# Attention with its row maxima shared between a front stage and the attention steps: 96 units in front in place of 80, and two maxima a step from step 171 on

## The chip, the cores and the metric

The kernel runs on one core of a Trainium2 chip. The time is the device time of one execution in microseconds, the median of several runs. Beside it stands the profile of one execution, whose span reaches from the program's first instruction to its last.

## What is computed

Two attention layers over the same input `x` (2048 tokens of 448 values, 16 heads of 28) and a gate that mixes them:

```
g = sigmoid((x * gate_w).sum(-1))
a = linear attention: phi(q) (phi(k)^T v) / (phi(q) phi(k)^T 1), phi = two softmaxes over a learned map
b = softmax(q k^T / sqrt(28)) v, all 2048 keys for every query
out = g * (a @ A_wo) + (1 - g) * (b @ B_wo)
```

The change is about layer b. Its softmax subtracts from every score the largest score of its query and head (the row maximum), so that the exponentials stay in range.

## The kernel before

**Order of the work.** The kernel writes out by hand the order of every instruction of TensorE (PE), VectorE (DVE), ScalarE (ACT) and GpSimd (POOL); each engine works through its own list in order. Transfers go through SyncE's queue (SP) and through scratch tensors in device memory. The stages are: the projections of queries and keys of layer b (`proj_qk`), the keys and values of layer a by tiles of 128 tokens (key stage, t = 0 to 15 of the loop at line 703), the queries of layer a and their products (the same loop, q = t - 16 from 0 on), the values of layer b (`value_b`, eight tiles in that loop from q = 18 on, eight behind it at line 926), and the attention of layer b (loop at line 1136).

**Attention.** There are 4 groups of 4 heads and 4 blocks of 512 queries, 16 pairs `gq` in all, and 16 tiles of 128 keys for each: 256 steps `s`. In a step `scores` (line 880) computes for each of the four heads a tile of 128 keys by 512 queries, in three passes (line 863; high and low parts of the numbers). The four heads lie in four groups of 32 rows of the PE array, so that four such matmuls run side by side. ACT turns each into exponentials (line 871). `values` (line 1001) multiplies the exponentials of two steps ago with the values (line 1008), eight passes that all run on all 128 rows. The row maximum enters the scores through an extra row of the query tile, so the maxima of a pair must be there before its first step: `load_nm` puts them there about four steps ahead.

**The row maxima** come from a cheaper computation of the same scores, and in two ways:

- *In the front*, `mx_unit` (line 238). A unit takes 128 queries, two heads and 1024 keys: four matmuls (line 260), in the four row groups; two give differences of the scores of two key tiles (`pmd`), two the scores of one of them (`pmb`). ACT takes the positive part of a difference (line 264), DVE adds it to the other score and takes the maximum over the row (line 265): two instructions on each. 16 units make a pair `gq`. A unit also issues the loads of what later units need: at certain units `pair_query` and `pair_load` (four and six transfers; the latter has a subtraction on POOL, taken up by `take_subs`), and towards the end `mx_query` and `mx_load`, the plain tiles for the second way.
- *In attention*, for the pairs that the front has left: the list `flats` (line 275), one item for 128 queries, one head and 512 keys. `mx_next` hands a step some items; `mx_score` (line 288) is one matmul of 28 rows in the row group of its head, `mx_done` one reduction on DVE (line 295). A unit of the front so replaces four items.

The split is `NF`, the number of units in front: 80 units do pairs 0 to 4; the other eleven pairs are 704 items, three to a step.

**Where the units stand in front** (80): one each in the last four of the `proj_qk` units; in the key stage, one at the start of each pair of tiles and three more from `tick`, which counts the matmul passes of the key and value tiles and starts a unit at each mark of `pace["at"]`; one at the start of iterations q = 0, 1 and of all from q = 8 on (line 747); a second at the end of iterations q = 19 to 25 (line 797); one at line 924; and the rest (`rest`, 15 units), spread over the 77 passes of value tiles 8 to 14. Banks: PSUM has eight, of 128 x 512 values. In the loop, units have four from q = 2 on, and six from the end of q = 22 on (`psn[1]`); a unit takes four of them.

**Banks in attention.** One bank is for the values, seven go round in `scores` by the list `free`. The order in which they are handed on to the next step is written there, one way for three maxima and another for any other number:

```
    if len(todo) == 3:
        b = free[:]
        free[:] = [b[2], b[0], b[3], b[1], b[6], b[4], b[5]]
        st, pm = {e0: b[0], e1: b[1], l0: b[4], l1: b[5]}, [b[2], b[3], b[6]]
    else:
        n = 4 + len(todo)
        b = free[:n]
        free[:] = free[n:] + b[4:] + b[:4]
        st, pm = dict(enumerate(b[:4])), b[4:]
```

`st` are the banks of the four scores, `pm` those of the maxima. With three maxima, the first passes of two heads (e0, e1) go out beside the maxima of the two others (l0, l1), whose scores follow one pass later. In the other branch the scores' passes come first, heads 0 to 3 in each, and the maxima last.

Of the kernel before, what the change touches and what calls it, by code (L numbers as in the profile page):

```python
# [24 lines left out]
NT = S // P  # L25
# [1 line left out]
SCALE = DH ** -0.5  # L27
EPS = 1e-6
NU = NG * NQ * 16
NF = 80  # L30
LOWEST = -3.0e38
LAG = 2
OUTS = (200, 238, 246, 210)
# [8 lines left out]
def gated_mix_kernel(ctx, tc, xT, wqkB, wvB, wvA, wkAT, wqAT, phi, woA, woB,  # L42
# [20 lines left out]
    def ps_s(nm):  # L63
        return ps.tile([P, 512], F32, tag="s", name=nm, bufs=psn[0])
# [4 lines left out]
    def ps_mx(nm):  # L69
        return ps.tile([P, 512], F32, tag="mx", name=nm, bufs=psn[1])  # L70
# [113 lines left out]
    def mx_load(g, c):  # L184
        mxs[("kc", g, c)] = mx_rows(mx_tile("kc", f"kc{g}_{c}", 5), range(4), k_d[g], range(4),
                                    c * 512)

    def mx_query(gq):
        g, qb = divmod(gq, NQ)
        mxs[("qc", gq)] = mx_rows(mx_tile("qc", f"qc{gq}", 3), range(4), q_d[g], range(4), qb * 512)  # L190
# [19 lines left out]
    def pair_query(gq, hp):  # L210
        g, qb = divmod(gq, NQ)
        mxs[("qp", gq, hp)] = mx_rows(mx_tile("qc", f"qp{gq}_{hp}", 3), range(4), q_d[g],
                                      (2 * hp, 2 * hp + 1) * 2, qb * 512)

    def mx_fin():
        while mxs["fin"]:
            mxs["fin"].pop(0)()

    GM = NF // 16

# [15 lines left out]
    def mx_unit():  # L238

        u = mxs["u"]  # L240
        if u == NF:
            return
        mx_fin()
        mxs["u"] = u + 1
        gq, r = divmod(u, 16)
        g, qb = divmod(gq, NQ)
        c, qt = divmod(r, 4)
        hp, b = divmod(c, 2)
        col = 64 * gq + 16 * b + 4 * qt + 2 * hp
        if r in (4, 9) and gq + 1 < GM:  # L250
            pair_query(gq + 1, r // 9)
        if r == 4 and gq + 1 == GM:
            mx_query(GM)
        qc, kc = mxs[("qp", gq, hp)], mxs[("kp", g, c)]

        pm = [ps_mx(f"pm{'ddbb'[j]}{u}_{j % 2}") for j in range(4)]
        for j in range(4):
            i = (j + 2) % 4
            js = slice(32 * i, 32 * i + DH)
            nc.tensor.matmul(pm[j], qc[js, qt * P:(qt + 1) * P], kc[js, :], start=True, stop=True,  # L260
                             tile_position=(32 * i, 0))
        for i in range(2):
            rl = rlp.tile([P, 512], F32, tag="rl", name=f"rl{u}_{i}", bufs=psn[2])
            nc.scalar.activation(rl, pm[i], AF.Relu)  # L264
            nc.vector.tensor_tensor_reduce(rl, pm[2 + i], rl, 1.0, LOWEST, ALU.add, ALU.max,  # L265
                                           part[:, col + i:col + i + 1])
        if gq + 1 < GM and qt == 3 and qb == NQ - 1:
            pair_load(g + 1, c)
        if gq + 1 == GM and qt == 3:
            mx_load(GM // NQ, c)  # L270
        if r == 15:
            mx_reduce(gq)


    flats = [(gq, kb, qt, h, 64 * gq + 16 * kb + 4 * qt + h) for gq in range(GM, NG * NQ)
             for qt in range(4) for kb in range(4) for h in range(4)]

    def mx_next():

        f = mxs["f"]  # L280
        todo = flats[f:f + 3]
        mxs["f"] = f + len(todo)
        return todo

# [403 lines left out]
    def value_b(t, mid=None):  # L688
        pv = ps_s(f"pvb{t}")
        tok_major(pv, t, wvB_s, D, mid)  # L690
        nc.scalar.copy(vb[t // 8][:, t % 8, :, 0:DH], pv[:, :D].rearrange("p (h d) -> p h d", d=DH))

    pace = {}
# [9 lines left out]
    for i in range(2 * NT + 11):  # L703
        t, q = i, i - NT
        y = q - 1
        tb = y // 2
        take_acts()
        if t < NT and t % 2 == 0:
            mx_unit()
            passes = (55 if t < NT - 4 else 44) + (4 if t >= 4 else 0)  # L710
            pace["n"], pace["at"] = 4 if t >= 4 else 0, [k * passes // 4 for k in range(1, 4)]
        if q in (0, 1):
            take_exps()

        if t % 2 == 0 and 0 <= t - 4 < NT:
            kv_add(t - 4)
            kv_add(t - 3)
        if q == 2:
            bk_s.close()
            ta_s = ExitStack()  # L720
            ta = ta_s.enter_context(tc.tile_pool(name="ta", bufs=1, reuse_waits="tile"))
            stg = ta_s.enter_context(tc.tile_pool(name="stg", bufs=2, reuse_waits="tile"))
            KV = ta.tile([P, 2, P], F32, name="KV")
            kvT = kv_copy()
            ps_s_.close()
            ps = ps_s_.enter_context(tc.tile_pool(name="psq", bufs=1, space=PSUM, reuse_waits="tile"))
            psn[0] = 4
            woA_s = weights(3, "woA_s")
            wvB_s = weights(2, "wvB_s")
            take_exps()  # L730
        if t < NT:
            pk = ps_s(f"pk{t}")
            tok_major(pk, t, wkA_s, D, tick)
            fk[t] = features1(pk, f"k{t}", nc.gpsimd)
            take_exps(1)
        if 0 <= q < NT:
            pq = ps_s(f"pq{q}")
            tok_major(pq, q, wqA_s, D)
        if q == 0:
            fk[NT - 1] = features2(fk[NT - 1], f"k{NT - 1}")  # L740
        if q in (1, 2):
            fq[q - 1] = features2(fq[q - 1], f"q{q - 1}")
        if 0 <= q < NT:
            fq[q] = features1(pq, f"q{q}", nc.vector if q in (4, 6) else nc.gpsimd)
        if 0 <= t - 1 < NT - 1:
            fk[t - 1] = features2(fk[t - 1], f"k{t - 1}")
        if q in (0, 1) or q >= 8:
            mx_unit()
        if y >= 6 and y % 2 == 0 and tb - 3 < 8:
            num[tb - 3] = normalize2(ta, *num[tb - 3], f"a{tb - 3}", 2)  # L750
        if y >= 9 and y % 2 and tb - 4 < 8:
            oTs[tb - 4] = normalize4(ta, num.pop(tb - 4), f"a{tb - 4}", 2)
        if q > 0:
            take_exps(int(q < NT))
        if q == 3:
            kv_out(kvT)
        if 2 <= q - 1 < NT:
            fq[q - 1] = features2(fq[q - 1], f"q{q - 1}")
        take_subs()
        if t == 1:  # L760
            pair_load(0, 3)
        if y >= 8 and y % 2 == 0 and y < NT and tb - 4 < 8:
            num[tb - 4] = normalize3(*num[tb - 4], 2)
        if t < NT:
            value_a(t)
            if t % 2 and t < NT - 4:
                proj_qk(NP + t // 2, ev)
        if q in (0, 1):
            proj_qk(NP + 6 + q, ev)
        take_lows()  # L770
        if 2 <= i < 6:
            fold(wqA_s, "q", i - 2)
        if q == 1:
            ev_s.close()
        if q == 2:
            part_loads("woA", woA, D, "woA")
            raws["wvB"] = [f32(ta.tile([P, 2, 512], F32R, tag="oT", name=f"wvB_raw{b}", bufs=4))[:, :, :D]
                           for b in (0, 2)]
            for i in range(2):
                nc.sync.dma_start(raws["wvB"][i], wvB[:, 2 * i:2 * i + 2, :])  # L780
        if q in (4, 6):
            split_part(woA_s, "woA", D, (q - 4) // 2, nc.gpsimd)
        if q in (8, 10):
            split_part(wvB_s, "wvB", D, (q - 8) // 2)
        if q == 1:
            gates()
        if y >= 4 and y % 2 == 0 and tb - 2 < 8:
            numer(tb - 2)
        if y < 9 or y % 2:
            if y >= 2 and y - 2 < NT:  # L790
                turn(y - 2)
        if 0 <= y - 10 < NT:
            out_a(y - 10)
            out_a2(y - 10)
        if y >= 9 and y % 2 == 0 and y - 2 < NT:
            turn(y - 2)
        if NT + 3 <= q < NT + 10:
            mx_unit()
        if y >= NT and y % 2 == 0 and tb - 4 < 8:
            num[tb - 4] = normalize3(*num[tb - 4], 2)  # L800
        if q == NT + 6:
            ps_s_.close()
            ps = ps_s_.enter_context(tc.tile_pool(name="psv", bufs=1, space=PSUM, reuse_waits="tile"))
            psn[:2] = 2, 6
        if q == NT + 2:
            bd_s.close()
            vb = [value_tile(0)]
        if 0 <= q - NT - 2 < 8:
            value_b(q - NT - 2)
    ta_s.close()  # L810
    wp_s.close()
    vb.append(value_tile(1))
# [2 lines left out]
    at = ctx.enter_context(tc.tile_pool(name="at", bufs=1, side="right", reuse_waits="tile"))  # L815
# [108 lines left out]
    mx_unit()  # L924
    rest = NF - mxs["u"]
    for t in range(8, NT):
# [8 lines left out]
        if t in (8, 12):  # L935
            load_k(0, t // 12)
    while mxs["u"] < NF:
        mx_unit()
# [197 lines left out]
    for s in range(NS + 18):  # L1136
# [28 lines left out]
        while vals and vals[0] <= upto:  # L1165
            t = vals.pop(0)
# [77 lines left out]
```

## Time and profile before

| | |
|---|---|
| median of 3 runs | 980.02 us (979.75 to 980.48) |
| the profiled execution | 979.64 us |
| its span | 977.9 us |
| granted TensorE clock | 1.00 throughout |

In the span, the key stage reaches from about 62 to 181 us, the query part and half of the values of layer b to 325, the rest of these values to 354, and attention to the end. In the timeline and the groups of the profile, a row names start and length (in the timeline), engine, line, operation, output<-input, shapes and count; in brackets stands the idle time ahead of it on its engine and what ended that. PEld is the loading of a matmul's stationary operand, which runs ahead of the matmul, and waits where the matmul's bank isn't free. A row of the table of stretches gives for each engine the busy time and, in parentheses, the count of instructions. The span's rows merge instructions of one kind that follow each other.

### The profile page before, as it was taken

Reading aid. Unit: us, or ns where it says so; the run is one execution under the profiler, and the core shown is the slowest. Engines: PE = TensorE matmul, PEld = TensorE weight load, DVE = VectorE, ACT = ScalarE, POOL = GpSimd, SP = SyncE. Lnnn points to the kernel's source line nnn. Section 1 sums busy time; section 2 is a strip of 40 time slices with the busy share of each in tenths; the row PEclk is TensorE's granted clock in tenths of the full one; section 3 lists DMA queues with packets and bytes.
Section 4 is the critical chain, followed back from the end, with each engine's and each line's share of the span. In section 5 each row is a group of like instructions: output and inputs, shape, how many; then the busy total and the mean of one; then the engine's idle time right before and its main releaser. Section 6 shows DMA issues by size and latency. Waiting matters only on the chain.

```text
span 977.9 us, 22543 instructions
## 1 busy us (share of the span) xinstructions
PE 970.2 (99%) x8510; PEld 600.8 (61%) x8510; DVE 715.9 (73%) x1338; ACT 751.8 (77%) x1442; POOL 227.4 (23%) x236
## 2 busy tenths in 40 slices
PE   9999999999999999999999999999999999999998
PEld 8877877787777655555555555555555555555555
DVE  5566767789745678888888888888888888885112
ACT  4455655578865689888898898988989889887662
POOL 1135435577634800021011001011011011010010
PEclk9999999999999999999999999999999999999999
DMA  9873110112243333022132121122231222100441
GB/s 305 310 256 113 39 53 33 37 52 82 75 114 108 98 112 132 29 59 50 60 91 73 33 61 47 59 77 72 65 83 45 63 60 64 42 21 32 142 151 57
DMA packets 56140, 84.49 MB, mean 86 GB/s; under 512 B 17216, under 2 KB 23984, under 8 KB 56032
## 3 DMA queue, kind: packets, MB, share of 16 engines
q1 hardware_dynamic: 56032, 83.06, 28.0%
q8 instruction: 67, 1.10, 0.5%
q14 instruction: 41, 0.34, 0.1%
HBM read 54.86 MB, written 27.78 MB: 85 GB/s over the span
## 4 chain that ended last, share of the span: by engine, by line
PE 93%; DMA 3%; DVE 2%; issue 1%; ACT 1%; SPq 1%; POOL 0%; DVEq 0%; POOLq 0%; ACTq 0%
PE g L863 29%; PE pv L1008 27%; PE pqk L109 5%; PE pk L127 4%; PE pva L127 4%; PE g L288 3%; PE poa L109 3%; PE pmd L260 3%; PE pob L109 3%; PE pq L109 3%; PE pvb L127 2%; PE pvb L109 2%; DMA rsa<-rda 2%; PE pqk L630 1%; PE pkv L468 1%
## 5 line engine op out<-in xcount | busy, mean ns | idle before, releaser
L871 ACT ACTIVATE p<-g 128x512 f32<-128x512 f32 x1020 | 525.6, 608 | 82.7 <-PE g L863 82.4
L295 DVE TENSOR_REDUCE part<-g 128x1 f32<-128x512 f32 x704 | 442.2, 683 | 84.0 <-PE g L288 82.8
L863 PEld LDWEIGHTS g<-qst,kst 32*128 32x128 f32 x3060 | 220.8, 182 | 215.5 <-DVE part L295 194.9
L863 PE MATMUL g<-qst,kst 32*128 32x512 f32 x3060 | 337.6, 419 | 0.1
L1008 PE MATMUL pv<-p,vb 128*32 128x512 f32 x2048 | 273.0, 604 | 0.0
L288 PE MATMUL g<-kc,qc 28*128 28x512 f32 x704 | 233.3, 494 | 0.0
L265 DVE CUSTOM_DVE_ANT_0 rl<-pmb,rl 128x512 f32<-128x512 f32 x160 | 103.3, 683 | 50.0 <-ACT rl L264 50.0
L400 POOL TENSOR_TENSOR oUb<-oUb,rsb 128x512 f32<-128x512 f32 x15 | 19.3, 1288 | 489.5 <-DMA rsb<-rdb 453.9
L264 ACT ACTIVATE rl<-pmd 128x512 f32<-128x512 f32 x160 | 87.4, 602 | 31.1 <-PE pmb L260 29.4
L288 PEld LDWEIGHTS g<-kc,qc 28*128 28x128 f32 x704 | 86.2, 181 | 0.2
L1008 PEld LDWEIGHTS pv<-p,vb 128*32 128x32 f32 x2048 | 40.5, 108 | 66.2 <-issue 64.9
L109 PE MATMUL pqk<-XH,wB 128*128 128x512 f32 x192 | 59.1, 396 | 0.0
L568 ACT CAST ev<-pqk 128x512 fp32r<-128x512 f32 x28 | 16.0, 589 | 39.1 <-PE pqk L109 23.0
L1019 DVE SCALAR_TENSOR_TENSOR acc<-pob,gate,acc 128x448 f32<-128x448 f32 x12 | 8.2, 683 | 48.4 <-PE pob L109 48.4
L109 PE MATMUL poa<-woA_s,oTa 128*128 128x448 f32 x192 | 43.5, 375 | 0.0
L260 PE MATMUL pmb<-kp,qp 28*128 28x512 f32 x160 | 41.7, 495 | 0.4
L569 DVE TENSOR_TENSOR ev<-pqk,ev 128x512 fp32r<-128x512 f32 x28 | 19.0, 690 | 30.4 <-ACT ev L568 30.3
L109 PEld LDWEIGHTS pqk<-XH,wB 128*128 128x128 f32 x192 | 35.4, 188 | 8.6 <-issue 1.5
L260 PE MATMUL pmd<-kp,qp 28*128 28x512 f32 x160 | 39.9, 494 | 0.0
L127 PE MATMUL pk<-wkA_s,XH 128*128 128x448 f32 x128 | 39.4, 381 | 0.0
L109 PEld LDWEIGHTS poa<-woA_s,oTa 128*128 128x128 f32 x192 | 34.8, 188 | 6.6 <-issue 2.6
L109 PE MATMUL pq<-wqA_s,XH 128*128 128x448 f32 x128 | 37.4, 375 | 1.4 <-ACT oUa L381 1.4
(158 smaller groups left out, 1053.9 us busy)
## 6 DMA issues: line engine op xcount, KB each, us to landing
qkd<-ev SPq DMA_DIRECT2D x28, 512.0 KB
qst<-qkd SPq DMA_DIRECT2D x64, 112.0 KB
kst<-qkd SPq DMA_DIRECT2D x64, 112.0 KB
od<-oTb SPq DMA_DIRECT2D x48, 112.0 KB
rsa<-rda SPq DMA_DIRECT2D x8, 512.0 KB
oL<-od SPq DMA_DIRECT2D x8, 512.0 KB
rsb<-rdb SPq DMA_DIRECT2D x15, 256.0 KB
gad<-ga SPq DMA_DIRECT2D x16, 224.0 KB
```

What stands on the lines that cost most here:

```text
L109: nc.tensor.matmul(dst, l, r, start=i == 0, stop=i == len(todo) - 1)
L127: nc.tensor.matmul(dst[:, :n], l, r, start=i == 0, stop=i == len(todo) - 1, skip_group_check=True)
L260: nc.tensor.matmul(pm[j], qc[js, qt * P:(qt + 1) * P], kc[js, :], start=True, stop=True, tile_position=(32 * i, 0))
L264: nc.scalar.activation(rl, pm[i], AF.Relu)
L265: nc.vector.tensor_tensor_reduce(rl, pm[2 + i], rl, 1.0, LOWEST, ALU.add, ALU.max, part[:, col + i:col + i + 1])
L288: nc.tensor.matmul(pm, mxs[("qc", gq)][js, qt * P:(qt + 1) * P], mxs[("kc", gq // NQ, kb)][js, :], start=True, stop=True, tile_position=(3 ...
L295: nc.vector.tensor_reduce(part[:, col:col + 1], pm, AX.X, ALU.max)
L400: (nc.gpsimd if n == 1 else nc.vector).tensor_mul(oU, oU, rs)
L569: nc.vector.tensor_sub(e[:, 1, :], pq, f32(e[:, 0, :]))
L863: nc.tensor.matmul(st[j], kst_of[(gq // NQ, kt // 4)][js, k, (kt % 4) * P:(kt % 4 + 1) * P], qst_of[gq][js, q, :], start=n == 0, stop=n == ...
L871: nc.scalar.activation(p, st[j], AF.Exp, scale=SCALE)
L1008: nc.tensor.matmul(pv[32 * j:32 * j + 32, :], vb[kt // 8][:, kt % 8, 4 * g + j, :], pt[j], start=kt == 0, stop=kt == NT - 1, tile_position ...
```

## The change

`NF` becomes 96: the front does pairs 0 to 5, and 640 items are left for attention. `mx_next` hands out three items for the first 170 steps that take any, then two. In the front there is a fourth mark in the key stage's pace, a second unit at the end of every iteration from q = 16 on, and a third in the middle of the value tiles of q = 22 to 25.

```diff
-NF = 80
+NF = 96
+THREES = 170
...
     def mx_next():
         f = mxs["f"]
-        todo = flats[f:f + 3]
+        todo = flats[f:f + (3 if f < 3 * THREES else 2)]
...
             mx_unit()
             passes = (55 if t < NT - 4 else 44) + (4 if t >= 4 else 0)
-            pace["n"], pace["at"] = 4 if t >= 4 else 0, [k * passes // 4 for k in range(1, 4)]
+            pace["n"], pace["at"] = 4 if t >= 4 else 0, [k * passes // 5 for k in range(1, 5)]
...
-        if NT + 3 <= q < NT + 10:
+        if q >= NT:
             mx_unit()
...
         if 0 <= q - NT - 2 < 8:
-            value_b(q - NT - 2)
+            value_b(q - NT - 2, (lambda k: mx_unit() if k == 5 else None) if q >= NT + 6 else None)
```

`NT` is 16. `value_b(t, mid)` calls `mid(k)` ahead of its pass k of eleven.

## The prediction

> **What bounds the kernel now.** I read the page's busy shares first, then its chain of work, then a table of stretches, then the timeline of single steps.
>
> ```profile
> span 977.9 us, 22543 instructions
> PE 970.2 (99%) x8510; PEld 600.8 (61%) x8510; DVE 715.9 (73%) x1338; ACT 751.8 (77%) x1442; POOL 227.4 (23%) x236
> ...
> PE 93%; DMA 3%; DVE 2%; issue 1%; ACT 1%; SPq 1%; POOL 0%; DVEq 0%; POOLq 0%; ACTq 0%
> ```
>
> TensorE carries the chain from end to end: whatever is added to its queue in the front is paid for, and attention is worth what a step takes on it. The timeline of the steps around the last row maxima shows what a step of each kind takes; the same view later shows steps without maxima.
>
> ```profile
> 889.37 1.06 PE L1008 MATMUL pv<-p,vb 128*32 128x512 f32 x8
> ...
> 891.66 1.07 PE L1008 MATMUL pv<-p,vb 128*32 128x512 f32 x8
> ...
> 892.66 0.97 PE L863 MATMUL g<-qst,kst 32*128 32x512 f32 x12
> ...
> 893.46 0.40 PE L288 MATMUL g<-kc,qc 28*128 28x512 f32 x2
> 893.73 2.06 ACT L871 ACTIVATE p<-g 128x512 f32<-128x512 f32 x4 [0.24 <-PE g L863]
> ...
> 893.79 1.06 PE L1008 MATMUL pv<-p,vb 128*32 128x512 f32 x8
> 893.90 1.29 DVE L295 TENSOR_REDUCE part<-g 128x1 f32<-128x512 f32 x2 [1.05 <-PE g L288]
> ...
> 894.79 1.42 PE L863 MATMUL g<-qst,kst 32*128 32x512 f32 x12
> ...
> 895.24 0.52 PEld L863 LDWEIGHTS g<-qst,kst 32*128 32x128 f32 x10 [0.27 <-DVE part L295]
> ...
> 896.13 1.07 PE L1008 MATMUL pv<-p,vb 128*32 128x512 f32 x8
> ```
> ```profile
> 933.90 1.06 PE L1008 MATMUL pv<-p,vb 128*32 128x512 f32 x8
> 934.89 0.97 PE L863 MATMUL g<-qst,kst 32*128 32x512 f32 x12
> 935.80 1.06 PE L1008 MATMUL pv<-p,vb 128*32 128x512 f32 x8
> ```
> ```profile
> 370.00:590.80 220.80, 220.80 (x2212) 115.28 (x2208) 187.15 (x310) 198.23 (x385) 21.52 (x22) 1.00 0.23 65
> ```
>
> A step runs from one group of value matmuls (L1008) to the next. With three maxima it takes 891.66 - 889.37 = 2.29 us; in the table, 2,212 matmuls in 220.8 us at 23 a step (12 scores, 8 value passes, 3 maxima) are 96 steps of 2.30 us, and I use 2.30. Without maxima it takes 935.80 - 933.90 = 1.90 us. The kernel before has one single step with two maxima, step 235, because 704 maxima are 234 threes and a pair: 893.79 - 891.66 = 2.13 us. The reader should not stop there. The step behind it has no maxima, yet takes 896.13 - 893.79 = 2.34 us, not 1.90: the weight loads of its third score wait until 895.24, released by DVE's reduction of the maxima of the step before. That is the wait on which this forecast rests.
>
> **The change: attention.** Steps 171 to 235, 65 of them, hold two maxima, not three (170 threes and 65 pairs are 640, and end at the same step 235). They use the other branch of `scores`. There the seven banks are handed on so: one bank that was unused, the two banks of the maxima, then the four of the scores. So the second and third score of a step write into the banks that the maxima of the step just before it occupied. The branch for threes (lines 885 to 890) hands on otherwise, and there the wait isn't seen: its second and third score take other banks, and DVE's part ends in time.
>
> With pairs in every step this becomes a loop: maxima on PE, two reductions on DVE, third score of the next step, its later passes, maxima. Its parts, all from the rows above: maxima's start to third score, 895.24 - 893.46 = 1.78 us (0.44 until DVE starts, 1.29 for the two reductions, 0.05 to reach PE). Then the third and fourth score do their first pass while the first two do their second, and so on; from 895.24 to the value group at 896.13 are 0.89 us, and the last pass starts 0.33 us ahead of it (893.79 - 893.46), 0.56 us after the third score. Maxima of heads 0 and 1 find their rows free at that point and run beside it: loop 1.78 + 0.56 = 2.34 us. Maxima of heads 2 and 3 follow the scores in the same rows, one pass later, 2.13 - 1.90 = 0.23: loop 2.57 us. The pairs alternate, since 510 leaves the list at head 2: 33 late and 32 early, 33 x 2.57 + 32 x 2.34 = 159.7 us. Before, the same steps took 64 x 2.30 + 2.13 = 149.3. **Attention: +10.4 us**, though it issues 64 PE and 64 DVE instructions fewer; were all pairs early or all late, +2.8 or +17.8. What is queued behind the waiting weight load: the fourth score, all second and third passes, the maxima, the values; and ACT's exponentials wait for those. ACT does not take over as the bound: four exponentials take 2.06 us. The end around step 236 is the same in both.
>
> [...]
>
> **The change: the front.** Sixteen more units (`mx_unit`: 4 PE, 2 ACT, 2 DVE instructions and 2 accumulator reads). Where they fall, counted from the code. Key stage: a fifth unit in each pair of tiles; but in the first two pairs the fourth mark is 4 x 55 // 5 = 44 and the counter reaches 43, so it falls in six pairs, not eight. Behind the queries: iterations q = 16, 17, 18 and 26 get a second unit, q = 22 to 25 a third, in mid value tile. That leaves rest = 17 where it was 15: two more among value tiles 8 to 14. 6 + 4 + 4 + 2 = 16. What one costs on PE where the engine is full:
>
> ```profile
> 84.70 0.57 PE L127 MATMUL pk<-wkA_s,XH 128*128 128x448 f32 x2
> 85.20 0.50 PE L260 MATMUL pmd<-kp,qp 28*128 28x512 f32 x2
> 85.20 0.50 PE L260 MATMUL pmb<-kp,qp 28*128 28x512 f32 x2
> 85.63 0.47 PE L127 MATMUL pk<-wkA_s,XL 128*128 128x448 f32 x1
> 85.94 0.36 PE L127 MATMUL pk<-wkA_s,XH 128*128 128x448 f32 x1
> ```
>
> Passes otherwise follow each other at 0.21 us (two take 0.57, one 0.36), so the second of the first row starts at 84.91. From there over the unit to 85.94 are 1.03 us for two passes: 1.03 - 0.42 = 0.61 us for the unit. 16 x 0.61 = **9.8 us**, if no bank is waited for. Now the banks. A unit takes four:
>
> ```profile
> 266.94 0.50 PE L260 MATMUL pmd<-kp,qp 28*128 28x512 f32 x2
> ...
> 268.07 1.15 ACT L264 ACTIVATE rl<-pmd 128x512 f32<-128x512 f32 x2
> ...
> 268.68 0.80 SPq L176 DMA_DIRECT2D qp<-qkd  x2
> 268.75 0.69 DVE L265 CUSTOM_DVE_ANT_0 rl<-pmb,rl 128x512 f32<-128x512 f32 x1 [0.39 <-ACT rl L264]
> ...
> 269.37 0.69 DVE L265 CUSTOM_DVE_ANT_0 rl<-pmb,rl 128x512 f32<-128x512 f32 x1
> 269.98 0.09 DVE L265 DVE_READ_ACCUMULATOR2_ANT part<- 128x1 f32 x1
> ```
> ```profile
> 324.87 0.50 PE L260 MATMUL pmd<-kp,qp 28*128 28x512 f32 x2
> ...
> 325.56 1.08 ACT L264 ACTIVATE rl<-pmd 128x512 f32<-128x512 f32 x2
> ...
> 326.50 0.50 PE L260 MATMUL pmd<-kp,qp 28*128 28x512 f32 x2
> 326.51 0.66 PE L260 MATMUL pmb<-kp,qp 28*128 28x512 f32 x2
> ```
>
> The first row's unit has its last bank back after 269.98 - 266.94 = 3.0 us; a unit that finds ACT free needs 0.50 for its matmuls and then the same 2.0 us (270.07 - 268.07): 2.5. Up to q = 22 there are four banks. The added unit of q = 16 and of q = 17 stands last in its iteration, and the next iteration begins with a unit: nothing between them on PE, so the second waits for the first's last bank. About 2.8 us more, between 2.5 and 3.0, in place of 0.61, twice: 5.6. Behind it in PE's queue stand the numerators and `out_a`. The same happens at q = 26, ahead of the unit at line 924, with six banks: there the last bank wanted is freed by the second relu (the lower rows: relus end 326.64, where the unit's last matmuls are held up until then), 1.8 us after the unit's start at 324.87: 1.8. At q = 18 it is 0.6. The four in mid value tile come 5 x 0.21 + 0.61 = 1.66 us after the one before, just at that limit of 1.8: 4 x 0.9 = 3.5. Key stage: 6 x 0.61 = 3.7, and where the marks are 9 or 10 passes apart (the last two pairs: 10 x 0.21 + 0.61 = 2.7 us against 2.5 to 3.0) some waiting: 1.3, an estimate from those two figures. The last 17: 77 passes, so every other gap is 4 passes (1.45 us) where the banks want about 1.65 (the two units of the lower rows stand 1.63 apart and the second is held only briefly): 1.2 for two units and 1.3 of waiting. Sum 5.6 + 1.8 + 0.6 + 3.5 + 5.0 + 2.5 = 19.0.
>
> Against it stands what these late units hide: in the iteration behind the queries DVE waits for a broadcast, and PE for the copy after it.
>
> ```profile
> 273.52 1.23 DVE L400 TENSOR_TENSOR oUa<-oUa,rsa 128x1024 f32<-128x1024 f32 x1 [3.19 <-DMA rsa<-rda]
> ...
> 276.35 0.67 PE L109 MATMUL pvb<-wvB_s,XH 128*128 128x448 f32 x2 [0.45 <-ACT fT L519]
> ```
>
> Only 0.45 us of that reached PE; it goes. **Front: +18.6 us**; bounds 16 x 0.43 = 6.9 (a unit's start to the next pass, 85.63 - 85.20, if nothing else were lost) and 23 (the 9 us of waiting half as much again). The queues: units carry their loads. Pair loads for head group 1 move from q = 20 to 26 up to q = 15 to 21, six DMAs on SP each, at 0.4 us (0.80 for two), past the broadcasts' own issues; one maximum query is replaced by two pair queries, four DMAs more in all. I cost this at nothing: each load is issued four or more iterations ahead of its use. If SP held the broadcast back by 2.4 us, that and the 0.45 are the price. POOL's subtractions ride along and have those iterations too.
>
> **Sum.** The profiled execution took 979.64 us (span 977.9 and 1.74 around it). 979.64 + 10.4 + 18.6 = 1008.6; the median of the runs is 0.4 above the profiled one, so **1009.0 us**.
>
> **Rivals.** *Steps of two at 2.13.* If the loop does not close, every pair costs what the single one did: 65 x (2.30 - 2.13) = -11.1, and with a front of +6.9 to +18.6 that is 976 to 988, 987.5 with mine. For it: the row of that step. Against it: the step after it, at 2.34. Chance 0.18. *The other side: the amount of emptying decides.* If PSUM is what paces and delays are hidden, a step falls to ACT's four exponentials or to a step without maxima, at 1.90 us: 65 x -0.40 = -26 us; with 18.6 in the front 973, with 9.8 about 964. It wins from where a step of two lasts under 2.30 - 18.6 / 65 = 2.01 us. Against it: in the table's 96 steps ACT is busy 198.2 of 220.8 us and DVE 187.2, so neither is full. [...] Chance 0.08. *The loop, but a front without bank waits:* 979.6 + 10.4 + 9.8 + 0.4 = 1000.2. For it: over all 80 units now, TensorE's loads for `pmb` waited 1.6 us for DVE.
>
> ```profile
> L260 PEld LDWEIGHTS pmb<-kp,qp 28*128 28x128 f32 x160 | 15.6, 181 | 1.6 <-DVE part L265 1.6
> ```
>
> Against it: those units stand apart, the new ones do not. Chance 0.14. *The change doing less than it says* is part of the count above (the two missing marks).
>
> **Numbers.** The forecast holds 0.60, between 1001 and 1016. 0.2%, some 2 us, is about what a measurement of this kernel can tell from none. Faster: 0.08 of the second rival and 0.02 of the first; the same: 0.03 of the first; slower 0.87. Range 985 to 1016: it leaves out the second rival, the lower half of the first, and a little above.
>
> **What would show it.** Value groups in steps 171 to 235 at 2.34 and 2.57 by turns, with the third score's weight load waiting for DVE L295; 2.13 throughout proves the first rival. Two units in a row near q = 16 to 18 with some 2.8 us between. Key stage six units longer by about 5 us. I am wrong if attention gets shorter, or if the front grows by under 8.

## The result, and the profile after

| | before | after |
|---|---|---|
| median | 979.75 us (978.63 to 980.48, 5 runs) | 1019.02 us (1018.05 to 1020.91, 5 runs) |
| profiled execution, span | 979.64 us, 977.9 us | 1018.34 us, 1016.6 us |
| mean granted TensorE clock in it | 1.000 | 0.997 |

The ratio is 1.0403 (95% interval 1.0388 to 1.0417): slower by 39 us, where 29 were forecast and the range ended at 36. The lines of the changed kernel are one higher (L261 for L260, L864 for L863, L1009 for L1008).

From the page of the changed kernel: the span, the busy shares, the row of granted clock in 40 slices, and the chain.

```profile
span 1016.6 us, 22751 instructions
PE 1004.7 (99%) x8510; PEld 595.3 (59%) x8510; DVE 699.2 (69%) x1338; ACT 769.6 (76%) x1474; POOL 228.5 (22%) x236
PEclk9999999999989999999999999999999999999999
PE 93%; DVE 2%; ACT 2%; issue 1%; DMA 0%; SPq 0%; POOL 0%; ACTq 0%; DVEq 0%; POOLq 0%
```

TensorE carries the chain as before, and DVE has less to do than before (699 us, not 716). One thing is new: an 8 in the row of the clock. To see where the time went, cut the span at the first group of value matmuls of attention; the timelines of before and of after have it here.

```profile
357.75 1.07 PE L1008 MATMUL pv<-p,vb 128*32 128x512 f32 x8
```
```profile
384.18 1.06 PE L1009 MATMUL pv<-p,vb 128*32 128x512 f32 x8
```

The front is 384.18 - 357.75 = 26.4 us longer (forecast 18.6). From there to the end are 1016.6 - 384.18 = 632.4 us, before 977.9 - 357.75 = 620.2: attention is 12.3 us longer (forecast 10.4).

**Attention.** The timeline of the changed kernel in two steps with two maxima each:

```profile
774.87 0.40 PE L289 MATMUL g<-kc,qc 28*128 28x512 f32 x2
...
775.19 1.06 PE L1009 MATMUL pv<-p,vb 128*32 128x512 f32 x8
775.36 1.29 DVE L296 TENSOR_REDUCE part<-g 128x1 f32<-128x512 f32 x2 [0.83 <-PE g L289]
...
776.70 0.53 PEld L864 LDWEIGHTS g<-qst,kst 32*128 32x128 f32 x10 [0.33 <-DVE part L296]
...
777.50 0.41 PE L289 MATMUL g<-kc,qc 28*128 28x512 f32 x2
...
777.84 1.06 PE L1009 MATMUL pv<-p,vb 128*32 128x512 f32 x8
777.93 1.29 DVE L296 TENSOR_REDUCE part<-g 128x1 f32<-128x512 f32 x2 [1.28 <-PE g L289]
...
779.27 0.53 PEld L864 LDWEIGHTS g<-qst,kst 32*128 32x128 f32 x10 [0.26 <-DVE part L296]
...
779.85 0.39 PE L289 MATMUL g<-kc,qc 28*128 28x512 f32 x1
...
780.17 1.07 PE L1009 MATMUL pv<-p,vb 128*32 128x512 f32 x8
```

Follow the loop by its starts: maxima 774.87, reductions 775.36, third score's weights 776.70 (released by DVE's reduction), maxima 777.50, reductions 777.93, third score 779.27, maxima 779.85. The step from 775.19 to 777.84 takes 2.65 us, the next to 780.17 takes 2.33, and so on by turns. The tables of stretches of before and of after give 65 steps, from the value group of step 171 to that of step 236 (matmuls in parentheses):

```profile
746.76:896.13 149.37, 149.37 (x1493) 77.16 (x1491) 126.01 (x209) 134.09 (x261) 12.68 (x12) 1.00 0.18 49
```
```profile
772.85:934.77 161.92, 161.63 (x1430) 61.54 (x1428) 88.56 (x145) 134.22 (x261) 12.89 (x13) 1.00 0.16 43
```

Each stretch begins behind the first two maxima and ends behind the step that follows the last, so it also holds that step's wait. 65 steps in 161.9 us, 2.49 each, with 63 matmuls fewer than the 65 steps of before in 149.4. The busy time of PE hardly shows the wait (161.63 of 161.92 us), since the scores of the first two heads run while the third waits: the twelve of one step take 1.49 us from 776.19 on, where the steps without the wait took 0.97.

**The front by stage.** The stages are cut at the starts of matmuls in the two timelines; a plus is time added, rounded.

| stage | measured | forecast |
|---|---|---|
| ahead of the key stage | +0.2 | 0 |
| key stage, first two pairs of tiles (no unit added) | +1.1 | 0 |
| key stage, four pairs in the middle (4 units) | +2.5 | +2.4 |
| key stage, last two pairs (2 units) | +5.7 | +2.5 |
| q = 0 to 15, up to the `out_a` shown below | -0.6 | 0 |
| from there to the first value tile, q = 16 to 18 (3 units) | +9.2 | +5.75 |
| q = 19 to 21 | 0.0 | 0 |
| q = 22 to 25 (4 units) | +3.7 | +3.5 |
| q = 26 and the rest (3 units) | +4.7 | +4.3 |

The forecast's 5.0 for the key stage is split here as it was worked out: 0.61 a unit, and 1.3 of waiting in the last two pairs; 5.75 is 5.6 + 0.6 - 0.45. Two stages are off by 3 us each. The first of them, units near the end of the key stage in the changed kernel:

```profile
170.81 0.50 PE L261 MATMUL pmd<-kp,qp 28*128 28x512 f32 x2
...
172.05 1.08 ACT L265 ACTIVATE rl<-pmd 128x512 f32<-128x512 f32 x2
...
172.40 1.08 DVE L450 TENSOR_REDUCE fsumk<-featk 128x32 f32<-128x896 f32 x1
...
173.50 0.50 PE L261 MATMUL pmd<-kp,qp 28*128 28x512 f32 x2
...
174.47 0.49 PE L261 MATMUL pmb<-kp,qp 28*128 28x512 f32 x1 [0.47 <-DVE part L266]
...
174.94 0.08 DVE L266 DVE_READ_ACCUMULATOR2_ANT part<- 128x1 f32 x1
...
175.16 0.49 PE L261 MATMUL pmb<-kp,qp 28*128 28x512 f32 x1 [0.20 <-ACT rl L265]
```

A unit starts 2.69 us after the one before, about the 2.7 of the forecast. But ACT starts on the first only 1.24 us after its matmuls (0.53 to 0.59 in the units of before from 158.34 to 176.91), and DVE then reduces key features for 1.08 us before it takes the unit's rows. So the first unit has its last bank back at 175.02, 4.2 us after its start, and the four matmuls of the second unit, which in the first all start at 170.81, go out from 173.50 to 175.16. In the kernel before, the units of these two pairs stand 3.1 us apart and have their last bank back after 2.5 to 3.1 us; with the fourth mark four of the ten have it after 3.6 or 4.2 us.

The second stage is q = 16 to 18. Before shows the `out_a` with which it begins (its end, the first value tile, stands in the prediction at 276.35); the changed kernel shows the same two and what lies between.

```profile
264.32 2.69 PE L109 MATMUL poa<-woA_s,oTa 128*128 128x448 f32 x12
```
```profile
273.26 2.69 PE L110 MATMUL poa<-woA_s,oTa 128*128 128x448 f32 x12
275.88 0.50 PE L261 MATMUL pmd<-kp,qp 28*128 28x512 f32 x2
...
277.70 0.99 PE L261 MATMUL pmd<-kp,qp 28*128 28x512 f32 x2 [1.32 <-ACT rl L265]
...
279.20 0.50 PE L261 MATMUL pmb<-kp,qp 28*128 28x512 f32 x1 [0.19 <-ACT rl L265]
279.63 1.85 PE L530 MATMUL pn<-fT,KV 57*32 57x256 f32 x32
281.42 3.54 PE L110 MATMUL poa<-woA_s,oTa 128*128 128x448 f32 x12
...
289.89 4.24 PE L110 MATMUL poa<-woA_s,oTa 128*128 128x448 f32 x12
...
294.49 0.67 PE L110 MATMUL pvb<-wvB_s,XH 128*128 128x448 f32 x2
```

The last matmul of the double's second unit goes out 279.20 - 275.88 = 3.3 us after the first began: the wait that was forecast, with 2.5 to 3.0. What was not forecast stands behind it: `pn` takes 1.85 us where it took 1.09 before, and twelve `poa` matmuls take 3.54 and 4.24 us in place of 2.7. The table of stretches of the changed kernel shows what came with it (the column behind the five engines is the granted clock):

```profile
276.40:279.80 3.40, 1.91 (x12) 0.90 (x20) 3.22 (x9) 2.93 (x6) 3.32 (x4) 1.00 0.39 124
279.80:283.20 3.40, 3.40 (x37) 2.15 (x24) 1.01 (x5) 1.07 (x2) 0.14 (x1) 0.50 0.35 115
...
286.70:290.10 3.40, 2.71 (x13) 1.79 (x14) 2.92 (x6) 2.57 (x5) 0.00 (x0) 0.99 0.75 161
290.10:293.50 3.40, 3.40 (x11) 3.03 (x10) 0.74 (x4) 1.73 (x5) 3.07 (x3) 0.50 0.30 98
```

Twice, right behind a stretch in which TensorE stood still for part of the time, it runs at half clock for 3.41 us. That is the 8 on the page. Before, it was 1.00 throughout.

### The profile page after: what moved, and what is told of

Same layout as the page of the kernel before. It is cut to its first block, busy times and chain, and to the rows that moved or that the text cites. A ratio compares the mean times of both kernels' runs of the same rounds, so it can differ in the third digit from the quotient of the medians.

```text
span 1016.6 us, 22751 instructions
## 1 busy us (share of the span) xinstructions
PE 1004.7 (99%) x8510; PEld 595.3 (59%) x8510; DVE 699.2 (69%) x1338; ACT 769.6 (76%) x1474; POOL 228.5 (22%) x236
## 3 DMA queue, kind: packets, MB, share of 16 engines
q1 hardware_dynamic: 56200, 83.29, 26.4%
## 4 chain that ended last, share of the span: by engine, by line
PE 93%; DVE 2%; ACT 2%; issue 1%; DMA 0%; SPq 0%; POOL 0%; ACTq 0%; DVEq 0%; POOLq 0%
PE g L864 30%; PE pv L1009 26%; PE pqk L110 5%; PE poa L110 4%; PE pk L128 4%; PE g L289 3%; PE pq L110 3%; PE pvb L128 3%; PE pmd L261 3%; PE pva L128 3%; PE pob L110 3%; PE pqk L631 1%; PE pvb L110 1%; DVE rl L266 1%; PE pft L517 1%
## 5 line engine op out<-in xcount | busy, mean ns | idle before, releaser
L296 DVE TENSOR_REDUCE part<-g 128x1 f32<-128x512 f32 x640 | 404.4, 685 | 134.6 <-PE g L289 129.8
L864 PEld LDWEIGHTS g<-qst,kst 32*128 32x128 f32 x3060 | 207.7, 183 | 234.5 <-DVE part L296 158.5
L864 PE MATMUL g<-qst,kst 32*128 32x512 f32 x3060 | 343.8, 426 | 0.3
L1009 PE MATMUL pv<-p,vb 128*32 128x512 f32 x2048 | 273.0, 605 | 0.0
L289 PE MATMUL g<-kc,qc 28*128 28x512 f32 x640 | 195.3, 474 | 0.0
L266 DVE CUSTOM_DVE_ANT_0 rl<-pmb,rl 128x512 f32<-128x512 f32 x192 | 124.0, 682 | 56.4 <-ACT rl L265 54.2
L265 ACT ACTIVATE rl<-pmd 128x512 f32<-128x512 f32 x192 | 106.2, 601 | 33.8 <-PE pmb L261 30.4
L1009 PEld LDWEIGHTS pv<-p,vb 128*32 128x32 f32 x2048 | 40.6, 108 | 73.6 <-issue 70.8
L289 PEld LDWEIGHTS g<-kc,qc 28*128 28x128 f32 x640 | 75.1, 182 | 1.5
L261 PE MATMUL pmb<-kp,qp 28*128 28x512 f32 x192 | 55.7, 495 | 2.8 <-ACT rl L265 1.6
L261 PE MATMUL pmd<-kp,qp 28*128 28x512 f32 x192 | 48.7, 494 | 2.3 <-ACT rl L265 2.3
L128 PE MATMUL pva<-wvA_s,XH 128*128 128x450 f32 x128 | 39.1, 377 | 0.0
```

The costliest lines, as they stand in the source:

```text
L128: nc.tensor.matmul(dst[:, :n], l, r, start=i == 0, stop=i == len(todo) - 1, skip_group_check=True)
L289: nc.tensor.matmul(pm, mxs[("qc", gq)][js, qt * P:(qt + 1) * P], mxs[("kc", gq // NQ, kb)][js, :], start=True, stop=True, tile_position=(3 ...
L296: nc.vector.tensor_reduce(part[:, col:col + 1], pm, AX.X, ALU.max)
L864: nc.tensor.matmul(st[j], kst_of[(gq // NQ, kt // 4)][js, k, (kt % 4) * P:(kt % 4 + 1) * P], qst_of[gq][js, q, :], start=n == 0, stop=n == ...
L1009: nc.tensor.matmul(pv[32 * j:32 * j + 32, :], vb[kt // 8][:, kt % 8, 4 * g + j, :], pt[j], start=kt == 0, stop=kt == NT - 1, tile_position ...
```

## The experiments

My theory after the result: attention is slower by the order in which banks change hands; the front by the units' 0.61 us, by waits where units stand close together, and by half clock behind such waits. The rivals: two maxima a step are slow as such; the step is set by the amount of emptying; the front is dear because of the loads that moved on SP; the added units have one price wherever they stand.

**Three maxima throughout, with the new front.** All 640 items go by threes and end at step 214.

```diff
-THREES = 170
+THREES = 1000
```

> The changed front (96 units), but three maxima in every attention step: the 640 maxima then end at step 214 and steps 215 to 235 have none. My theory (front and attention cost apart, and the loss in attention is the loop through the maxima's banks): the front stays 26 us longer than before, steps with three stay at 2.30 us, and 21 steps at 1.90 in place of 2.30 give 8.4 us back: about 997.5 us. Rival (attention is slower because the longer front leaves something behind, loads or a lower clock): steps stay slow and it is 1010 us or more.

Measured: 999.51 us, ratio 1.0207 (1.0191 to 1.0223). The steps with three take 2.30, those without 1.96. The profiled execution is the slowest of the four (1001.55 us), and most of what it has above the expectation lies in its front, which is 3.1 us longer than the changed kernel's: 10.2 us from 349.1 on are at half clock, too, again behind a stretch with TensorE busy 2.80 of 3.40 us. Attention takes 612.5 us in its trace. So going to two from step 171 on costs 19.5 us by the medians (19.9 in attention, by the two traces) against staying at three, and the new front doesn't pay with threes either.

**Another order of banks for pairs.** The amount of work is the same. The second and fourth score of a step now take banks that scores of the step before had; the third takes the bank of the first maxima, which DVE empties first, and the bank of the second maxima goes to maxima again.

```diff
-            free[:] = free[n:] + b[4:] + b[:4]
+            if n == 6:
+                free[:] = [free[6], b[0], b[4], b[1], b[2], b[5], b[3]]
+            else:
+                free[:] = free[n:] + b[4:] + b[:4]
```

> The changed kernel with one edit: a step with two maxima hands its banks on so that the next step's scores take the unused bank, the first score's, the first maximum's and the second score's, and the next maxima the third score's and the second maximum's. The same instructions in the same order. My theory (the third score waits for DVE's second reduction through the bank): pairs of steps at 2.34 and 2.64 us become 2.13 to 2.2 each, 65 steps give back 19 to 23 us: 996 to 1000 us. Rival (the pass order of this branch or the engines' work sets the step): within 3 us of 1019.

Measured: 996.89 us, ratio 1.0186 (1.0168 to 1.0203). Its table of stretches for the same 65 steps, and its timeline around one of them:

```profile
771.40:911.34 139.94, 139.94 (x1431) 59.48 (x1429) 88.48 (x145) 134.21 (x260) 12.83 (x13) 1.00 0.18 50
```
```profile
777.84 1.06 PE L1012 MATMUL pv<-p,vb 128*32 128x512 f32 x8
777.94 1.29 DVE L296 TENSOR_REDUCE part<-g 128x1 f32<-128x512 f32 x2 [0.90 <-PE g L289]
778.83 0.59 PEld L864 LDWEIGHTS g<-qst,kst 32*128 32x128 f32 x12 [0.84 <-ACT p L872]
...
780.03 1.06 PE L1012 MATMUL pv<-p,vb 128*32 128x512 f32 x8
```

All twelve weight loads of the scores now go out in one row at 778.83, while DVE still reduces (until 779.23). A step takes 2.15 us (139.94 / 65), by turns 2.12 and 2.19: nearly the 2.13 of the single pair before. The 22.0 us from 161.9 to 139.9 are the order of banks: the count of matmuls and the busy times of DVE and ACT are those of the changed kernel. This ends the rivals on pairs as such and on the amount of emptying.

**The new attention alone, with the front of before.** 80 units; 64 items of the last pairs are left out of the list to get to 640, so that the row maxima of query blocks 12 to 15 are taken over three quarters of the keys.

```diff
+THREES = 170
...
-             for qt in range(4) for kb in range(4) for h in range(4)]
+             for qt in range(4) for kb in range(4 if gq < 12 else 3) for h in range(4)]
...
-        todo = flats[f:f + 3]
+        todo = flats[f:f + (3 if f < 3 * THREES else 2)]
...
-        if qt == 3 and kb == 3:
+        if qt == 3 and kb == (3 if gq < 12 else 2):
             mx_reduce(gq)
```

> The front of the kernel before (80 units) and the attention of the changed one (170 steps with three maxima, 65 with two). So that the counts fit, 64 maxima are left out: those over the last 512 keys for query blocks 12 to 15, so their row maximum is over three quarters of the keys. My theory: only the loop in the steps with two is lost, 12.3 us: 992 us, with a span of attention as in the changed kernel. Rival (what the step of two saves is real and the changed front spoils it): 969 to 980 us.

Measured: 991.73 us, ratio 1.0125 (1.011 to 1.014): +12.7 us to the 979.04 of the kernel before on the same chip, and 162.06 us for the 65 steps. Attention's part doesn't depend on the front.

**No added unit at q = 16 and 17.** They go to the last value tiles (19 there).

```diff
-        if q >= NT:
+        if q >= NT + 2:
```

> The changed kernel without the added units in iterations q = 16 and 17, which stand directly ahead of the next iteration's unit; the last value tiles take up the two units (19 in place of 17). My theory: the stall of some 2.7 us between each two units goes, and with it the two stretches of 3.4 us at half clock that follow them: iterations 16 to 18 are 8.6 us shorter, the last value tiles 2 to 2.5 us longer: 1012 to 1013 us, clock at 1.00 there. Rival (the clock falls for another reason, the longer load): the two stretches at half clock stay and it is 1015 us or more.

Measured: 1017.29 us, ratio 1.039 (1.0375 to 1.0406): a miss by 4 us. Where I looked for the gain it came: from the `out_a` above to the first value tile are 12.7 us (12.0 before, 21.2 in the changed kernel), at full clock. The tail took 1.9 of it, as expected. The rest, 4.8 us, went to a place that I had not thought of, the value tiles of q = 23 to 25. From its timeline and its table of stretches:

```profile
323.73 1.23 DVE L401 TENSOR_TENSOR oUa<-oUa,rsa 128x1024 f32<-128x1024 f32 x1 [2.70 <-DMA rsa<-rda]
```
```profile
324.60:328.00 3.40, 2.77 (x11) 1.47 (x10) 2.89 (x9) 2.33 (x5) 0.50 (x1) 1.00 0.29 103
328.00:331.40 3.40, 3.40 (x11) 2.11 (x10) 2.31 (x7) 2.58 (x5) 2.82 (x4) 0.51 0.18 67
```

DVE stood 2.70 us waiting for a broadcast (`rsa`) to land, then did its normalization; behind both stood its work for the units, so that one in mid value tile waited for its banks. TensorE was busy 2.77 of 3.40 us, and 6.8 us of half clock followed, from 328.0 on. So half clock isn't bound to the doubles. Why the broadcast came so late beside TensorE's work here is not shown.

**The last pairs of key tiles with three marks, not four.** Their two added units go to the last value tiles (19).

```diff
-            pace["n"], pace["at"] = 4 if t >= 4 else 0, [k * passes // 5 for k in range(1, 5)]
+            pace["n"], pace["at"] = 4 if t >= 4 else 0, [k * passes // n for n in [4 if t >= 12 else 5] for k in range(1, n)]
```

> The changed kernel, but the last two pairs of key tiles (t = 12 to 15) keep the three marks of before; the last value tiles take up the two units (19 in place of 17). In the changed kernel these two pairs, up to the first query tiles, are 5.7 us longer than before for two units more. My theory (the fourth mark sets units 2.5 us apart, nearer than the 3.6 us after which DVE, busy with the key features, frees their last bank): that stretch gets its old length back, -5.7 us; the last value tiles cost 2 us more: 1015 us, give or take 2 for stretches at half clock. Rival (a unit costs what it costs wherever it stands, and the wait only moves): within 1.5 us of 1019, and the stretch gets back no more than 1.2 us.

Measured: 1015.02 us, ratio 1.0358 (1.0341 to 1.0376). The two pairs, from their first `pk` to the first `pq`, in the changed kernel and in this one:

```profile
160.35 0.68 PE L128 MATMUL pk<-wkA_s,XH 128*128 128x448 f32 x2
...
190.41 0.67 PE L110 MATMUL pq<-wqA_s,XH 128*128 128x448 f32 x2
```
```profile
159.82 0.68 PE L128 MATMUL pk<-wkA_s,XH 128*128 128x448 f32 x2
...
184.20 0.67 PE L110 MATMUL pq<-wqA_s,XH 128*128 128x448 f32 x2
```

30.06 against 24.38 us, the length of before: the two units cost 5.7 us here and 2.0 in the tail, as expected.

**The first two pairs with the marks of before.** The same edit, with `t < 4` for `t >= 12`.

> The changed kernel, but the first two pairs of key tiles (t = 0 to 3) keep the marks of before at passes 13, 27 and 41 in place of 11, 22 and 33 (the fourth, at 44, is never reached). No unit moves to another stage. In the changed kernel these two pairs are 1.1 us longer than before with the same units. My theory (nearer marks meet banks not yet free): they get 1.1 us back: 1018 us. Rival (noise, or the loads of these tiles): they stay as long as in the changed kernel.

Measured: 1016.88 us, ratio 1.0388 (1.0365 to 1.041). By times alone that is not told from the changed kernel; the trace settles it. The two pairs take 31.5 us, 32.6 in the changed kernel and 31.5 before: the 1.1 us are the marks, which put the same units elsewhere among the key features. This trace also has 3.4 us of half clock from 61.5 on, ahead of the key stage and so of every unit that the change adds or moves.

**Doubles alone, in the kernel before.** A unit right behind another at q = 20, 23 and 25, and 12 in the last value tiles, not 15.

```diff
         if NT + 3 <= q < NT + 10:
             mx_unit()
+            if q in (NT + 4, NT + 7, NT + 9):
+                mx_unit()
```

> The kernel before with three of its front units taken from the last value tiles (12 in place of 15) and each put directly behind another unit, at the ends of iterations q = 20, 23 and 25. The same units, attention untouched. My theory: each such unit holds TensorE for 2.5 to 2.8 us at q = 20 (four banks) and 1.5 to 1.8 at q = 23 and 25 (six banks), and where TensorE so stands still in a window of 3.4 us, the next window or windows run at half clock for about 1.5 us more each. 6 us for the three units less 3 us saved at the end, and one to three windows: 984 to 988 us, clock below 1.00 right behind those places. Rival (the low clock of the changed kernel has to do with its other work, its length or its transfers): clock at 1.00 up to the end and 981 to 983 us.

Measured: 985.98 us, ratio 1.0057 (1.004 to 1.0074). The profile's clock is 1.00 throughout, which I had not expected, so it shows a double without half clock:

```profile
287.94 0.50 PE L260 MATMUL pmd<-kp,qp 28*128 28x512 f32 x2
...
289.23 0.99 PE L260 MATMUL pmd<-kp,qp 28*128 28x512 f32 x2 [0.78 <-ACT rl L264]
...
290.65 0.49 PE L260 MATMUL pmb<-kp,qp 28*128 28x512 f32 x1 [0.20 <-ACT rl L264]
```

With four banks (q = 20) the iteration is 2.7 us longer than before, with six (q = 23 and 25) 1.8 each: the forecast's 2.8 and 1.8. The same program's other three executions had clocks of 0.997 and 0.998 and took 985.65 to 986.50 us, the profiled one 983.37. So a double costs its wait without half clock, too, and some executions have half clock on top. Where it stood in those three is not on record; one of seven executions of the kernel before had it as well (981.34 us at 0.998).

**All repairs together.** The order of banks, no added unit at q = 16 and 17, three marks in the first two and the last two pairs; 21 units in the last value tiles.

```diff
-            pace["n"], pace["at"] = 4 if t >= 4 else 0, [k * passes // 5 for k in range(1, 5)]
+            pace["n"], pace["at"] = 4 if t >= 4 else 0, [k * passes // n for n in [4 if t < 4 or t >= 12 else 5] for k in range(1, n)]
...
-        if q >= NT:
+        if q >= NT + 2:
...
-            free[:] = free[n:] + b[4:] + b[:4]
+            if n == 6:
+                free[:] = [free[6], b[0], b[4], b[1], b[2], b[5], b[3]]
+            else:
+                free[:] = free[n:] + b[4:] + b[:4]
```

> The changed kernel with the repairs together: banks handed on as in e2_banks, no added units in iterations q = 16 and 17, the marks of before in the first two and the last two pairs of key tiles; the last value tiles take up the units (21 in place of 17). My theory: attention 9 us shorter than before, the front 17 to 19 us longer (2.5 in the key stage, 1 behind the queries, 4 among the first value tiles, 7.5 at the last ones, the rest for stretches at half clock): 986 to 990 us, so it doesn't beat the kernel before. Rival (the costs of the front were only stalls and go with them): 975 to 980 us.

Measured: 986.33 us, ratio 1.0071 (1.0054 to 1.0088). Its first value group:

```profile
373.36 1.06 PE L1012 MATMUL pv<-p,vb 128*32 128x512 f32 x8
```

The front is 15.6 us longer than before's, attention (984.1 - 373.36 = 610.7) 9.4 us shorter: 33 of the 39 us are got back, and the kernel is still 7 slower than before. By these numbers a better place alone doesn't turn the account: 16 units at the 0.61 us that one costs where nothing waits are 9.8 us, and this attention gives 9.4 back. A place where a unit costs less, or an order of banks that gives back more, was not tried.

## Why the prediction was wrong, point by point

The direction and the loop were right, the sum was 10 us short: 7.8 in the front, 1.9 in attention, the rest the medians. Two steps failed, both in the front and by some 3 us each: the waiting for banks at the end of the key stage was put at 1.3 us and was 4.5, and the doubles were priced at full clock. With 26.4 us the front lies above the 23 that were its upper bound, too.

- **Bound on TensorE: right.** The chain's share is 93% before and after.
- **Attention, the loop: right, a little short.** Forecast were 2.57 and 2.34 us by turns with the third score waiting for DVE; the typical steps are 2.63 and 2.34. The late step's loop is 777.50 - 774.87 = 2.63: 1.83 to the third score (forecast 1.78; DVE starts 0.49 us after the maxima, not 0.44) and 0.80 from there (0.79). 33 times 0.06 is the 2 us. The other order of banks shows that the wait is the cause. One reading of the code was not right: in the branch for threes the third score does take a bank of maxima, the third one's, and the first score that of the first (`b[6]` and `b[2]`); but the third goes out one pass later, and its steps take 2.30 us.
- **First rival, 2.13 a step: a true price, for a loop that doesn't close.** The kernel with the other order has nearly that (2.15); the changed one has the loop.
- **Second rival, the amount of emptying: fell.** With DVE as busy in both (88.6 and 88.5 us), 65 steps take 161.9 us in the one order of banks and 139.9 in the other.
- **The unit at 0.61 us: right where nothing waits.** The four middle pairs of key tiles grew by 0.60 to 0.64 each.
- **"Some waiting: 1.3" in the last pairs of key tiles: the first step that failed.** It took a bank's way back as 2.5 to 3.0 us wherever a unit stands. That held for the marks of before, here too (2.5 to 3.1), but the fourth mark puts units where ACT and DVE are in the midst of the key features, and the way back becomes 3.6 to 4.2 us, with units about as far apart as forecast. Two units cost 5.7 us, not 2.5, so 4.5 of waiting; with three marks all of it goes. That the first two pairs would be as before, since no unit is added there, failed as well: moved marks cost 1.1.
- **The doubles at q = 16 and 17: the wait right, the clock the second step that failed.** Kernels with the same doubles had one or two half-clock stretches here: from the `out_a` to the first value tile are 19.6 us with one (the kernel with three marks at the end of the key stage, where the twelve `poa` behind the first double take 2.71 us, those behind the second 4.06) and 21.2 with two, so some 1.6 each. Taken off, 18.0 remain, 6.0 more than before; 5.75 were forecast. The forecast took every matmul at full clock, since the profile of before showed nothing else. Whether the 0.45 us of its gain are in it can't be told: with the front of before, unchanged up to there, this stretch takes 12.0 us in one run and 11.4 in two others.
- **The middle of value tiles, q = 26, the last tiles: right** (+3.7 for 3.5, where 4 x 0.9 would be 3.6, and +4.7 for 4.3).
- **Loads moved ahead on SP: right at nothing.** q = 19 to 21, where the normalization uses the broadcasts behind those loads, took as long as before. In the kernel without the first two doubles a broadcast did hold up DVE for 2.70 us.
- **The third rival, a front without bank waits, fell:** 26.4 us, not 9.8.

## What to carry to other kernels

Moving work off a stage is priced at both ends by the engine that carries the chain: here a unit costs 0.61 us of TensorE in front where nothing waits, and gives back 0.59 in attention (9.4 / 16) with the better order of banks, so that better placement alone has nothing to win. Count how late a bank comes back for the very moment at which the added work starts, by laying it against what ACT and DVE do then: the same stage gave 2.5 or 4.2 us. Where the number of buffers in a rotation changes, look at who had each buffer last: order alone was worth 22 us.

## What the runs showed of the hardware

Half clock came behind stretches in which TensorE was idle for only a part: it was busy 1.91 and 2.71 of 3.40 us ahead of the two stretches in the changed kernel, 2.77 in the kernel without those doubles. The stretches at half clock lasted 3.41 us in the changed kernel, 6.8 in the one without those doubles, 3.4 and 10.2 with threes throughout, and within one run their starts lie whole multiples of 3.41 us apart (279.8 and 290.1 are three; in the run with the early marks 61.5, 280.0 and 351.7 are 64 and 21). One program can have half clock in one execution and not in another: with the doubles in the kernel before, the mean clock was 1.000 in one and 0.997 or 0.998 in three. What makes the difference is not shown. Over executions of one program the price is plain: with the early marks 1016.7 to 1017.0 us at a mean clock of 0.997, and 1020.9 at 0.993.

The busy share doesn't decide alone: the changed kernel has this stretch, 16 times 3.41 us behind 290.1, with the next one at full clock, where in two other kernels (with threes throughout and with the early marks) half clock followed a stretch with 2.80 of 3.40 us.

```profile
344.70:348.10 3.40, 2.80 (x17) 1.94 (x16) 1.46 (x5) 1.80 (x5) 1.87 (x3) 1.00 0.00 0
348.10:351.50 3.40, 3.40 (x15) 1.96 (x15) 3.04 (x10) 2.36 (x5) 3.12 (x6) 1.00 0.26 86
```

Nor does the length of the wait: at the first double TensorE stands still for 1.32 us ahead of the second unit and for 0.19 ahead of its last matmul, both in the changed kernel and in the one with three late marks, and behind it `pn` takes 1.85 us in the first and 1.09 in the second. And with threes throughout half clock lasted three stretches, though TensorE was busy throughout the first two (3.40 of 3.40 us). What sets the clock stays open.
